# Last stage of a fused attention and expert kernel: the order of row turning, fetches, splits and SiLU work

## The chip, the cores and the metric

The kernel runs on one core of one Trainium2 chip. The metric is device microseconds of one launch, from inputs in HBM to the output in HBM. The core has a matrix engine (TensorE, "PE" in the rows), VectorE ("DVE"), ScalarE ("ACT"), GpSimd ("POOL") and the queue of SyncE ("SP") that issues most DMAs. TensorE reads weights with a separate load instruction ("PEld") that runs beside its products.

## What is computed

Three parts follow one another, all in float32, for 4 x 576 = 2304 rows of width 512:

```
p_packed = softmax_attention(p, k, v)          # 32 packed queries per head
x  = softmax_attention(q, p_packed, p_packed)  # as rows (2304, 512)
x  = sum over the 2 best of 8 experts of gate * (relu(x @ w1[e]) @ w2[e])
h  = x @ w_in                                  # 512 -> 2048
out = (h * sigmoid(h)) @ w_out                 # 2048 -> 512
```

The last two lines are the last stage, and the change touches that stage alone.

## The kernel before

To keep the precision of float32 on TensorE, every operand is held as two parts, a rounded high part and a low part ("rest" = value minus high part), and every product is three matmuls: high x high, high x rest, rest x high. ScalarE makes a high part by copying, VectorE or GpSimd the rest by subtracting. In the names of the rows a last letter h or l stands for these two.

Before the last stage, experts run one after the other (`expert_block`, line 259) and store their rows to a DRAM tensor `ys`. A row tile of the last stage (128 rows; there are 18) is fetched by two indirect DMAs of GpSimd from `ys` (`gather`, 866), gated, that is, scaled and added by ScalarE and VectorE (`gated`, 874), and turned, that is, transposed in four pieces by TensorE (`tps` in the rows) and copied out of PSUM. Fetched tiles come from a ring of five.

The last stage has two forms.

**Two blocks** of two row tiles (tiles 0 to 3; `final_block`, 837). Each has 16 steps f: a first product (12 matmuls of 256 columns, `hps<-` in the rows), the SiLU of the result (`silu_split`, 820: ScalarE's sigmoid, VectorE's product, ScalarE's high part, GpSimd's rest), the second product of the step but one before (6 matmuls of 512 columns, `acc<-`; the list `pend` with `flush`, 248, keeps it that far behind), and a hook (1302, 1308). The hook of the first block still loads and splits the output weights. Through `early(s)` (1275), with s = f in the first block and 16 + f in the second, the hooks also bring in the rows of what follows: tiles 2 and 3 for the second block, and tiles 4 to 11 for the first group. Row j is gathered at s = 1 + 2j, and gated and turned together at s = 4 + 2j. From s = 18 the turned rows of the first group are combined and split (`refill`, 918): seven operands, called 11, 21, t2, t1, t3, t4 and 22, written where the input weights of the second block were. The first pair of weights is loaded at s = 22 (`pair_load`, 964) and split at s = 26 and 28 (`pair_in`, 978).

**Two groups of super blocks** (`super_blocks`, 1046): the first group has eight row tiles (512 columns per product), the second six (384 columns). Each group has eight super blocks p = 0 to 7, one pair of hidden blocks each. A super block forms the first layer by seven products (`prod<-`) in place of eight, in Strassen's manner; sums of products are made by VectorE and GpSimd between them (u2, u3, p1, p5 and c11 in the code; `ul`, `uh` and `c` in the rows), and four SiLUs (h11, h21, h22, h12) come out. The products write two PSUM banks in turn, so a product waits until the product before last has been read. Between the products stand the output products of the super block before: chunks a0 to a3 (`acc<-`) and b0 to b3 (`y2p<-`, summed by VectorE), with j below 4 in the first group and below 3 in the second. Chunks a need h11 and h21, chunks b need h12 and h22.

During the first group the rows of the second are brought in: `rows_in` (892) gathers ahead, and one `row_in` (882) in three parts (gating; turning; copy) goes through each super block from p = 1, where p = 0 issues only the first gather; the row that is left at the end of p = 5 is done there in one go (1171). `mixed` (905) forms sums at p = 6, and `refill` splits the seven operands at p = 7: one at each of five places, and the last two at the end (1175).

**What sets the order.** From the last stage on (`M["fin"]`) every call on an engine keeps program order on that engine (`Kept`, 45). Generators are advanced with `next` at fixed places of the code, and that is the whole schedule. Engines run beside one another and wait by semaphores; an instruction that waits holds all behind it on its engine. Wrapped calls all appear under line 57, so the rows are told apart by tile names.

Of the kernel before, what the change touches and what calls it, by code (L numbers as in the profile page):

```python
# [7 lines left out]
F32 = mybir.dt.float32  # L8
# [11 lines left out]
P = 128  # L20
# [43 lines left out]
def body(ctx: ExitStack, tc: tile.TileContext, q, k, v, p, wg, wn, noise, w1, w2, w_in, w_out, out):  # L64
# [706 lines left out]
    def routed():  # L771
        ctx = mx = ExitStack()
        with mx:
# [63 lines left out]
            def final_block(m, x, hook):  # L837
                t0, n = BLOCKS[m]
                acc = [None]

                def step2(f, h):
                    if f == 0:
                        acc[0] = [pa.tile([P, DM], F32, name="acc", tag="acc") for _ in range(n)]
                    second(acc[0], h, wo, f, 15, 0)
                    if f == 15:
                        for j, y in enumerate(acc[0]):
                            store(t0 + j, A if j % 2 else V, y)
                for f in range(16):
                    ps = first(wi, x, f, n * P)
                    h = silu_split(ps, n * P)  # L850
                    flush(M["lag"])
                    pend.append(lambda f=f, h=h: step2(f, h))
                    hook(f)
# [25 lines left out]
            def staging(tags):  # L879
                box["st"] = [xp_.tile([P, 4, BW], F32, name="st", tag=tag) for tag in tags]  # L880

# [36 lines left out]
            def refill(st, xq, w, mix=None):  # L918
# [3 lines left out]
                def put(nm, src):  # L922
# [3 lines left out]
                    if type(src) is list:  # L926
                        for c in range(2):
                            A.activation(hi[:, c], src[c], AF.Copy)
                            V.tensor_tensor(lo[:, c], src[c], hi[:, c].bitcast(F32), op=OP.subtract)
                    else:  # L930
                        A.activation(hi, src, AF.Copy)
                        V.tensor_tensor(lo, src, hi.bitcast(F32), op=OP.subtract)
                    xq[nm] = [hi, lo]
                put("11", b11)
                yield
                put("21", b21)
                yield
                if mix:
                    t1, t2 = mix
                else:  # L940
                    t1 = b11
                    t2 = [mo.tile([P, DM], F32, name="t2", tag="ysb", bufs=3)[:, 0:w] for _ in range(2)]
                    V.tensor_tensor(t1, b12, b11, op=OP.subtract)
                    for c in range(2):
                        V.tensor_tensor(t2[c], b22[:, c], t1[:, c], op=OP.subtract)
                put("t2", t2)
                yield
                if mix:
                    V.tensor_tensor(b21, b21, t2, op=OP.subtract)
                else:  # L950
                    for c in range(2):
                        V.tensor_tensor(b21[:, c], b21[:, c], t2[c], op=OP.subtract)
                put("t1", t1)
                yield
                if not mix:
                    V.tensor_tensor(b12, b22, b12, op=OP.subtract)
                put("t3", b12)
                yield
                put("t4", b21)
                yield  # L960
                put("22", b22)
                yield
# [63 lines left out]
            def silu(src, h):  # L1026
# [6 lines left out]
                M["sv"] = V.tensor_tensor(src, src, sg, op=OP.mult)  # L1033
                M["sa"] = A.activation(h[0], src, AF.Copy)
# [11 lines left out]
            def super_blocks(xq, win, ro):  # L1046
# [4 lines left out]
                for g in range(last + 1):  # L1051
# [31 lines left out]
                    if g == last:  # L1083
                        next(late, None)
                        for c in ("a0", "a1", "b0", "a2", "b1", "a3", "b2", "b3"):
                            chunk(c)()
# [4 lines left out]
                    if more and p == 0:  # L1091
                        box["rows"] = rows_in(*SUPER[k + 1], ("xha", "xla"))
                    if more and p == 6:
# [16 lines left out]
                    next(late, None)  # L1110
                    next(fill, None)
                    next(wo_now)
                    if more and p < 7:
                        rows = next(box["rows"], none)
# [7 lines left out]
                    h11 = next(s11)  # L1122
                    next(s11)
# [28 lines left out]
                    next(s22)  # L1152
                    V.tensor_tensor(u3, ps, u3, op=OP.add)
                    next(fill, None)
                    s21 = silu(u3, low())
                    h21 = next(s21)
                    e = chunk("a3")
# [3 lines left out]
                    next(s21)  # L1161
# [9 lines left out]
                    if more and p == 5:  # L1171
                        for r in box["rows"]:
                            for _ in r:
                                pass
                    if p == 7 and more:
                        for _ in fill:
                            pass
                        xq = nxt
# [96 lines left out]
            def early(s):  # L1275

                j, odd = divmod(s - 1, 2)
                if not odd and 0 <= j < 2 + 2 * n0:
                    inflight[j] = gather(2 + j)
                j, odd = divmod(s - 4, 2)  # L1280
                if not odd and 0 <= j < 2 + 2 * n0:
                    y = inflight.pop(j)
                    if j < 2:
                        transposed(plain(gated(2 + j, y)), *X["c"], j)
                    else:
                        if j == 2:
                            staging(("xhb", "xlb"))
                        for _ in row_in(2 + j, y, box["st"], n0, j - 2):
                            pass
                if s == 18:  # L1290
                    win.append(refill(box["st"], xq, w0))
                if s in (18, 20, 23, 25, 27, 29, 31):
                    next(win[0], None)
                if s == 22:
                    win.append(pair_load(0))
                if s == 26:
                    win.append([])
                    win.append(pair_in(0, win[1][0], win[2]))
                if s in (26, 28):
# [14 lines left out]
            super_blocks(xq, win[2][0], win[1][1])  # L1314
# [110 lines left out]
```

## Time and profile before

| | us |
|---|---|
| median of 3 runs | 1032.12 (1029.96 to 1033.7) |
| profiled execution, its own time | 1035.61 |
| span in its profile | 1033.8 |
| TensorE busy | 962.2 (93%) |
| VectorE busy | 638.6 (62%) |
| ScalarE busy | 436.6 (42%) |
| GpSimd busy | 369.4 (36%) |
| mean granted TensorE clock | 0.97 |

Times are counted from the start of the span. The two blocks run from about 578 to 708 us, the first group from 708 to 877, the second from 877 to the end. Matmuls are pipelined, so a busy TensorE isn't one at its peak; a stall shows as an idle time in brackets, with the engine that ended it. The granted clock is a share of full speed: 1.0 is 2.4 GHz and 0.5 is 1.2 GHz.

### The profile page before, as it was taken

The numbers are of one execution on the slowest core, as the hardware profiler recorded it, in microseconds if no ns is written. First come the engines' busy times: TensorE is split into PE (matmuls) and PEld (weight loads), VectorE is DVE, ScalarE is ACT, GpSimd is POOL, SyncE is SP. The second block draws the span as 40 slices with busy tenths as digits, with TensorE's granted clock in tenths as the row PEclk, the third lists the DMA queues.
The fourth block names the chain that finished last, engine by engine and source line by source line (L and its number), as shares of the span: only waits on it lengthen the run. The fifth ranks groups of instructions, "written<-read, shape, count | busy, mean of one in ns | idle before, by whom it ended". The sixth has DMA issues, their size and how long they took to land.

```text
span 1033.8 us, 15376 instructions
## 1 busy us (share of the span) xinstructions
PE 962.2 (93%) x5716; PEld 830.4 (80%) x5716; DVE 638.6 (62%) x1157; ACT 436.6 (42%) x804; POOL 369.4 (36%) x385
## 2 busy tenths in 40 slices
PE   6999799899999999999999967798999989899997
PEld 4767678799999999999999856686788876788885
DVE  4537576567667676767444542266777777877773
ACT  3566423343434343433333443444544434544442
POOL 2163212734425161524001143424454533434442
PEclk8989899999999999999999979999999999999999
DMA  9994414575767575756233542202222211412111
GB/s 246 242 243 132 130 55 126 176 251 186 224 202 226 179 244 165 240 188 223 93 113 123 190 144 64 83 21 81 82 77 66 82 41 42 142 42 82 53 30 65
DMA packets 103554, 139.35 MB, mean 135 GB/s; under 512 B 17200, under 2 KB 66352, under 8 KB 103472
## 3 DMA queue, kind: packets, MB, share of 16 engines
q1 hardware_dynamic: 95504, 117.57, 36.5%
q0 software_dynamic: 7520, 19.93, 6.7%
q8 instruction: 47, 0.77, 0.3%
q10 hardware_dynamic: 448, 0.79, 0.2%
q14 instruction: 35, 0.29, 0.1%
HBM read 109.94 MB, written 28.31 MB: 134 GB/s over the span
## 4 chain that ended last, share of the span: by engine, by line
PE 71%; DVE 11%; ACT 6%; issue 4%; POOL 3%; DMA 3%; SPq 1%; ACTq 0%; POOLq 0%; DVEq 0%
PE acc L57 8%; PE hps L231 7%; PE hps L232 7%; PE hps L233 7%; PE acc L244 7%; PE acc L242 7%; PE acc L243 7%; PE prod L57 6%; PE hps L57 4%; PE y2p L57 4%; DVE ul L57 2%; DVE sm L57 2%; ACT sg L57 2%; POOL gl L57 2%; DVE y L57 1%
## 5 line engine op out<-in xcount | busy, mean ns | idle before, releaser
L199 POOL DMA_INDIRECT xg<-xs,idx x120 | 129.4, 1079 | 179.6 <-DVE xturn L208 145.8
L255 ACT ACTIVATE hh<-hps 128x384 fp32r<-128x384 f32 (+1 forms) x128 | 56.1, 438 | 259.3 <-PE hps L233 205.4
L256 DVE SCALAR_TENSOR_TENSOR hl<-hps,hh 128x384 fp32r<-128x384 f32 (+1 forms) x128 | 62.4, 487 | 107.2 <-ACT hh L255 92.1
L57 POOL TENSOR_TENSOR gl<-sg,gh 128x256 fp32r<-128x256 f32 x32 | 26.9, 843 | 87.4 <-ACT gh L57 58.1
L57 DVE TENSOR_TENSOR ul<-ul,sg 128x512 f32<-128x512 f32 (+1 forms) x32 | 26.8, 837 | 24.3 <-ACT sg L57 24.3
L57 PE MATMUL y2p<-wb5h,g 128*128 128x512 f32 x112 | 39.3, 393 | 0.2 <-POOL g L57 0.2
L57 PE MATMUL y2p<-wb4h,g 128*128 128x512 f32 x112 | 39.3, 391 | 0.0
L57 DVE TENSOR_TENSOR sg<-hps,sg 128x256 f32<-128x256 f32 x32 | 13.5, 422 | 41.5 <-ACT sg L57 41.5
L57 POOL TENSOR_TENSOR gl<-ul,gh 128x512 fp32r<-128x512 f32 (+1 forms) x16 | 30.5, 1904 | 20.4 <-ACT gh L57 20.4
L57 POOL DMA_INDIRECT y<-ys,slots x32 | 31.9, 998 | 12.3 <-DMA raw<-wf_out 5.2
L57 DVE TENSOR_TENSOR y<-y,y2p 128x512 f32<-128x512 f32 x42 | 28.6, 681 | 12.5 <-PE y2p L57 12.5
L57 POOL TENSOR_TENSOR g<-uh,g 128x512 fp32r<-128x512 f32 (+1 forms) x16 | 20.7, 1293 | 38.7 <-ACT g L57 38.7
L57 PE MATMUL tps<-ident,y 128*128 128x128 f32 x64 | 10.9, 297 | 24.4 <-DVE y L57 24.4
L57 ACT ACTIVATE sg<-ul 128x512 f32<-128x512 f32 (+1 forms) x32 | 18.5, 579 | 34.1 <-POOL ul L57 33.9
L219 POOL DMA_INDIRECT xg<-xs,idx x10 | 9.9, 992 | 60.9 <-DVE hl L256 28.9
L57 PEld LDWEIGHTS tps<-ident,y 128*128 128x128 f32 x64 | 7.6, 150 | 29.8 <-issue 26.2
L813 POOL DMA_INDIRECT y<-ys,slots x4 | 4.6, 1157 | 73.4 <-DVE hl L256 72.5
L57 POOL TENSOR_TENSOR ul<-ul 128x512 f32<-128x512 f32 (+1 forms) x16 | 19.1, 1192 | 32.0 <-DVE ul L57 32.0
L57 POOL TENSOR_TENSOR g<-ul,g 128x512 fp32r<-128x512 f32 (+1 forms) x16 | 19.0, 1189 | 31.4 <-ACT g L57 20.6
L57 PE MATMUL acc<-wb5h,gl 128*128 128x512 f32 x64 | 25.9, 405 | 4.5 <-POOL gl L57 4.5
L57 POOL TENSOR_TENSOR gl<-c,gh 128x512 fp32r<-128x512 f32 (+1 forms) x16 | 18.5, 1157 | 28.3 <-ACT gh L57 23.0
L57 PE MATMUL acc<-wb4h,gl 128*128 128x512 f32 x64 | 25.6, 400 | 2.7 <-POOL gl L57 2.7
(686 smaller groups left out, 3479.8 us busy)
## 6 DMA issues: line engine op xcount, KB each, us to landing
raw<-in_moe_w_dram SPq DMA_DIRECT2D x56, 512.0 KB
raw<-wf_out SPq DMA_DIRECT2D x24, 512.0 KB
ys<-ysb SPq DMA_DIRECT2D x40, 256.0 KB
raw<-in_moe_w_in_dram SPq DMA_DIRECT2D x16, 512.0 KB
raw<-in_moe_w_out_dram SPq DMA_DIRECT2D x16, 512.0 KB
raw<-wf_in SPq DMA_DIRECT2D x32, 256.0 KB
xs<-xr SPq DMA_DIRECT2D x18, 256.0 KB
km<-in_k_dram SPq DMA_DIRECT2D x8, 512.0 KB
```

The costliest lines, as they stand in the source:

```text
L57: ins = fn(*args, **kw)
L199: G.indirect_dma_start(out=xg[:, g * P:(g + 1) * P], out_offset=None, in_=xs[:, :].rearrange("n (a f) -> (n a) f", a=4), in_offset=bass.In ...
L219: G.indirect_dma_start(out=xg[:, :], out_offset=None, in_=src, in_offset=bass.IndirectOffsetOnAxis(ap=ix[:, c:c + 1], axis=0))
L231: T.matmul(ps, wh[:, c, s], xh[:, c, :n], start=c == 0, stop=False)
L232: T.matmul(ps, wh[:, c, s], xl[:, c, :n], start=False, stop=False)
L233: T.matmul(ps, wl[:, c, s], xh[:, c, :n], start=False, stop=c == 3)
L242: T.matmul(y, hh[:, s], wh[:, f % 2, :], start=f == 0, stop=False)
L243: T.matmul(y, hh[:, s], wl[:, f % 2, :], start=False, stop=False)
L244: T.matmul(y, hl[:, s], wh[:, f % 2, :], start=False, stop=f == last)
L255: A.activation(hh, ps, AF.Relu)
L256: V.scalar_tensor_tensor(hl, ps, 0.0, hh.bitcast(F32), op0=OP.max, op1=OP.subtract)
L813: G.indirect_dma_start(out=y[c][:, :], out_offset=None, in_=src, in_offset=bass.IndirectOffsetOnAxis(ap=slots[:, t, c:c + 1], axis=0))
```

## The change

In the two blocks, row j is gathered at s = 2 + 2j, gated at s = 5 + 2j and turned at s = 6 + 2j, so gating and turning stand in different steps. At the very first step both pending second products of the last expert are flushed. The parts of the first group's `refill` are spread over single steps; its last two splits (t4 and 22) move into the first super block, which takes the generator as `fill0`. The first pair of weights is loaded at s = 19 and split at s = 22 and 24. The first fetch of the second group is issued at s = 24, and its rows go through p = 0 to 5.

In the second group's `refill`, a rest is made one place after its high part, and the rests of 21, t3 and 22 are GpSimd's; the last two splits are made in the next group's first super block. In every super block the sum u3 stands ahead of the SiLU product of h22, and the high part and rest of h21 ahead of those of h22. After the last super block, the b chunk of the last tile comes third instead of last.

```
 final_block
-                    flush(M["lag"])
+                    flush(0 if f == m == 0 else M["lag"])
...
 refill: put
-                        V.tensor_tensor(lo, src, hi.bitcast(F32), op=OP.subtract)
+                        e = G if mix and nm in ("21", "t3", "22") else V
+                        rest.append(lambda: e.tensor_tensor(lo, src, hi.bitcast(F32), op=OP.subtract))
+                        if not mix:
+                            rest.pop()()
...
+                rest = []
+                def again():
+                    if rest:
+                        rest.pop(0)()
                 put("11", b11)
                 yield
+                again()
                 put("21", b21)
                 yield
                 if mix:
+                    again()
                     t1, t2 = mix
+                    put("t2", t2)
+                    yield
+                    again()
+                    put("t1", t1)
+                    yield
+                    again()
+                    V.tensor_tensor(b21, b21, t2, op=OP.subtract)
+                    put("t3", b12)
...
                 yield
+                again()
                 put("t4", b21)
                 yield
+                again()
                 put("22", b22)
+                yield
+                again()
                 yield
...
 silu
-                M["sv"] = V.tensor_tensor(src, src, sg, op=OP.mult)
-                M["sa"] = A.activation(h[0], src, AF.Copy)
+                V.tensor_tensor(src, src, sg, op=OP.mult)
+                yield
+                A.activation(h[0], src, AF.Copy)
                 G.tensor_tensor(h[1], src, h[0].bitcast(F32), op=OP.subtract)
                 yield
...
 super_blocks
-                        for c in ("a0", "a1", "b0", "a2", "b1", "a3", "b2", "b3"):
+                        for c in ("a0", "a1", f"b{prev['n'] - 1}", "a2", "a3", "b0", "b1", "b2")[:5 + prev["n"] - 1]:
...
-                    if more and p == 0:
+                    if p == 0:
+                        fill = fill0
+                    if g and more and p == 0:
                         box["rows"] = rows_in(*SUPER[k + 1], ("xha", "xla"))
+                        next(box["rows"])
...
-                    if more and p < 7:
-                        rows = next(box["rows"], none)
+                    if more and p < 6:
+                        rows = next(box["rows"])
                         next(rows, None)
...
                     ps = product(wt["t4"], x["t4"])
                     e()
-                    next(s22)
                     V.tensor_tensor(u3, ps, u3, op=OP.add)
-                    next(fill, None)
                     s21 = silu(u3, low())
                     h21 = next(s21)
+                    next(s22)
+                    next(s21)
+                    next(s21)
+                    next(s22)
+                    next(fill, None)
                     e = chunk("a3")
                     e2 = chunk("b2")
                     ps = product(wt["22"], x["22"])
                     e()
-                    next(s21)
                     e2()
...
-                    if more and p == 5:
-                        for r in box["rows"]:
-                            for _ in r:
-                                pass
                     if p == 7 and more:
-                        for _ in fill:
-                            pass
-                        xq = nxt
+                        fill0, xq = fill, nxt
...
 early
-                j, odd = divmod(s - 1, 2)
-                if not odd and 0 <= j < 2 + 2 * n0:
-                    inflight[j] = gather(2 + j)
-                j, odd = divmod(s - 4, 2)
+                j, odd = divmod(s - 6, 2)
                 if not odd and 0 <= j < 2 + 2 * n0:
                     y = inflight.pop(j)
                     if j < 2:
-                        transposed(plain(gated(2 + j, y)), *X["c"], j)
+                        transposed(plain(y), *X["c"], j)
                     else:
                         if j == 2:
                             staging(("xhb", "xlb"))
-                        for _ in row_in(2 + j, y, box["st"], n0, j - 2):
-                            pass
+                        turn_in(y, box["st"], n0, j - 2)
+                j, odd = divmod(s - 5, 2)
+                if not odd and 0 <= j < 2 + 2 * n0:
+                    inflight[j] = gated(2 + j, inflight[j])
+                j, odd = divmod(s - 2, 2)
+                if not odd and 0 <= j < 2 + 2 * n0:
+                    inflight[j] = gather(2 + j)
                 if s == 18:
                     win.append(refill(box["st"], xq, w0))
-                if s in (18, 20, 23, 25, 27, 29, 31):
+                if s == 24:
+                    box["rows"] = rows_in(*SUPER[1], ("xha", "xla"))
+                    next(box["rows"])
+                if s in (18, 20, 25, 26, 27, 28, 29, 30, 31):
                     next(win[0], None)
+                if s == 19:
+                    win.append(pair_load(0))
                 if s == 22:
-                    win.append(pair_load(0))
-                if s == 26:
                     win.append([])
                     win.append(pair_in(0, win[1][0], win[2]))
-                if s in (26, 28):
+                if s in (22, 24):
                     next(win[3])
```

`turn_in` is the new name of the turning and copying half of `row_in`. Where `refill` has no `mix` (the first group), its sums and splits are the same, with a `yield` between each.

## Rows read from the trace of the kernel before

**Rows 1.** Windows: stretch, length, busy PE, PEld, DVE, ACT, POOL, clock, DMA share, GB/s.
```profile
592.90:707.60 114.70, 91.95 (x543) 80.61 (x544) 47.66 (x68) 47.14 (x92) 43.95 (x50) 0.93 0.26 79
707.60:730.90 23.30, 19.29 (x72) 14.30 (x71) 16.57 (x21) 11.43 (x19) 9.90 (x8) 0.85 0.29 90
853.00:876.80 23.80, 21.64 (x91) 16.41 (x90) 17.67 (x25) 10.17 (x17) 7.25 (x5) 1.00 0.14 44
876.80:901.30 24.50, 20.75 (x91) 17.55 (x92) 21.81 (x30) 14.09 (x24) 11.14 (x8) 0.93 0.35 118
```

**Rows 2.** Waits of TensorE (total, times, longest): 578 to 707.6, 731 to 901.3, 901.3 to 1030.
```profile
PE tps L57 <- DVE y L57: 20.9, 10, 3.6
...
PE tps L57 <- DVE y L57: 2.6, 1, 2.6
...
PE acc L57 <- POOL gl L57: 5.8, 7, 0.9
```

**Rows 3.** Timeline, one row turned in the first block (start us, us, engine; idle before).
```profile
635.93 1.02 DVE L57 SCALAR_TENSOR_TENSOR y<-y,gates,y 128x512 f32<-128x512 f32 x1 [1.10 <-ACT y L57]
637.10 0.63 PE L57 MATMUL tps<-ident,y 128*128 128x128 f32 x4 [1.82 <-DVE y L57]
637.49 0.36 PE L57 MATMUL hps<-xha,wa6h 128*128 128x256 f32 x1
```

**Rows 4.** Chain that ended last, a step without a row turned (start us, us, what).
```profile
682.45 1.43 PE hps L57 x12
683.88 1.39 PE acc L57 x6
```

**Rows 5.** Timeline, the first row's fetch and its gating.
```profile
590.64 0.96 POOL L57 DMA_INDIRECT y<-ys,slots  x1 [5.21 <-DMA raw<-wf_out]
591.90 0.95 POOL L57 DMA_INDIRECT y<-ys,slots  x1 [0.30 <-issue]
596.84 0.70 ACT L57 ACTIVATE y<-y,gates 128x512 f32<-128x512 f32 x1
```

**Rows 6.** Timeline around the first super block and the first row of the next.
```profile
704.92 1.04 ACT L57 ACTIVATE wa6h<-st 128x1024 fp32r<-128x1024 f32 x1
709.21 0.59 ACT L57 ACTIVATE uh<-prod 128x512 f32<-128x512 f32 x1
709.34 1.23 DVE L57 TENSOR_TENSOR wb4l<-raw,wb4h 128x1024 fp32r<-128x1024 f32 x1 [1.50 <-ACT wb4h L57]
728.86 1.30 DVE L57 SCALAR_TENSOR_TENSOR y<-y,gates,y 128x512 f32<-128x512 f32 x1 [0.39 <-ACT y L57]
730.31 0.63 PE L57 MATMUL tps<-ident,y 128*128 128x128 f32 x4 [0.91 <-DVE y L57]
```

**Rows 7.** Chain that ended last, one first-layer product of each group.
```profile
745.95 1.36 PE prod L57 x6
...
906.27 1.04 PE prod L57 x6
```

**Rows 8.** Timeline, h21 in one super block of the second group.
```profile
914.28 0.33 PE L57 MATMUL prod<-wa5h,wb2l 128*128 128x384 f32 x1
914.33 0.53 ACT L57 ACTIVATE sg<-ul 128x384 f32<-128x384 f32 x1 [1.50 <-POOL ul L57]
915.36 0.55 DVE L57 TENSOR_TENSOR ul<-prod,ul 128x384 f32<-128x384 f32 x1
918.20 1.90 POOL L57 TENSOR_TENSOR gl<-ul,gh 128x384 fp32r<-128x384 f32 x1 [1.11 <-ACT gh L57]
920.15 0.50 PE L57 MATMUL acc<-wb5h,gl 128*128 128x512 f32 x1 [0.90 <-POOL gl L57]
```

**Rows 9.** Groups by form (xcount, busy, mean ns, idle before): GpSimd 730 to 1030, VectorE 900 to 1020.
```profile
L57 POOL TENSOR_TENSOR gl<-c,gh 128x384 fp32r<-128x384 f32 x8 | 8.2, 1020 | 11.6 <-ACT gh L57 11.6
...
L57 DVE TENSOR_TENSOR c<-c,sg 128x384 f32<-128x384 f32 x7 | 3.9, 559 | 4.1 <-ACT sg L57 4.1
```

**Rows 10.** Timeline, ScalarE's queue at the end: two half stores of the last row tile.
```profile
1028.23 1.18 ACTq L862 DMA_DIRECT2D out_dram<-osb  x2
```

## What the change should do to the time

> **What bounds the kernel now.** I read the stretches of the last stage first: share of TensorE and granted clock in each. Four of them hold idle or half-clock time [rows 1]. Then TensorE's waits, by stage: three causes recur [rows 2]. Then the timeline around one instance of each, to see what the late engine did just before.
>
> In the two first blocks (592.9 to 707.6 us) TensorE waits 20.9 us, ten times, for VectorE's y, once per row turned [rows 2]. One instance shows the order: ScalarE's scaling of y, VectorE's 1.02 us sum, the transposes 1.82 us late, and the next step's first product only 0.39 us after the transposes begin [rows 3]. All stand at the end of one step and in program order, so TensorE can't overtake. With no row to turn a step lasts 2.82 us, 1.43 us for the first product and 1.39 for the second of an earlier one [rows 4]. So that stretch needs 27 steps x 2.82 = 76.1, two last second products at 1.39 [rows 4] = 2.8, the rest of a step begun earlier 0.9 (four of its six matmuls) and ten transpose groups x 0.39 = 3.9: **83.7 us**. It takes 114.7, so 31.0 us are lost: 20.9 in these waits, the rest mostly in steps at the lower clock level (mean granted clock 0.93 there, of which 1.0 is 2.4 GHz and 0.5 is 1.2 GHz) [rows 1].
>
> **The change, part by part.**
>
> *Rows a step behind their gates.* Gather moves from step 1 + 2j to 2 + 2j, gating from 4 + 2j to 5 + 2j, turning to 6 + 2j. Nothing is added: ten rows, the same gathers, gatings, transposes. The y that ends 1.02 + 0.15 us before the transposes today would end a full 2.82 us step earlier, so the 1.82 us wait has 1.0 us in hand. What is late next? The gather still has three steps to its gate, about 8.5 us once no step is stretched; the row of the first gather ends issuing at 592.85 and ScalarE uses its data at 596.84 without a recorded wait, 4.0 us later [rows 5]: enough. GpSimd's order is rest of the SiLU, then two gathers (0.95 us each and 0.3 between [rows 5]); the first product of a step reaches its own second product two steps later, so the rest may come some 3 us late. The tiles of a fetch are a ring of five, so the second gather of row j + 2 waits for the transposes of row j in the same step; they come before GpSimd gets there. The first fetch comes one step later, and the last expert's stores, whose products move ahead of one first product, 1.43 us earlier; so what is left of today's 5.21 us in GpSimd's queue [rows 5], with the SiLU rest queued behind it, is about 1 us. Weight loads for the second product keep their step, but steps are shorter, so a load that is issued two steps ahead has about 5.7 us; ScalarE may wait there at a few steps. SP is passed by one pair of weight loads (step 22 to 19) whose tiles are free by then. Ends: -31 (every loss gone) to -20 (loads and gathers bind in a third of the steps); I take **-28**, near the whole, as the dense steps at 682 us carried all the splits of the second block. Those splits (earlier weight pair in steps 22 and 24, sums and splits one to a step from 25) cost nothing: VectorE is busy 47.66 of 114.7 us here [rows 1] and no step gets more than its 2.82 us but step 22, whose excess of a few tenths is caught up in the next. The same holds for the first fetch of the second group at step 24, 2.2 us of GpSimd.
>
> *Two splits and the first row moved into the first super block.* This adds to a stage where VectorE is the bottleneck (16.57 of 23.3 us busy, clock 0.85 [rows 1]). Each split is a ScalarE copy of 1.04 us and a VectorE rest of 1.23 (a weight rest of the same width), the gating 1.30 us on VectorE [rows 6]. Counted from the first product's start at 707.6 [rows 1]: its copy out ends at +2.2 as now (709.80 [rows 6]); the split's copy then +3.3, its rest +4.5, the weight rest (1.23) +5.8, the gated row +7.0. TensorE has finished two products (1.36 each [rows 7]) at +2.8 and now meets the transposes: a new wait of **4.2 us**, with five products queued behind it. The second split holds the sum that frees a bank for the fifth product 1.23 us more, a second wait of about 2.5. Part of this replaces today's own waits there. Following the queue on, the next super block reaches its transposes at about +26.5, against 730.31 - 707.6 = +22.7 now [rows 6]. Ends: 0 (the work slips under existing idle time, and the low clock is as long as today) to +8 (the 4.2 us again at the lower clock). I take **+4**.
>
> *The row left for the end of step 5* no longer waits: **-2.6** [rows 2].
>
> *Change of group.* Its two super blocks take 23.8 and 24.5 us [rows 1]; dense they need 15 x 1.36 = 20.4 and 7 x 1.04 + 8 x 1.39 = 18.4 [rows 4, 7], so 9.5 us are lost. Seven rests on VectorE become four, three go to GpSimd, and two of the seven operands are split in the next super block instead of all at the border, each rest one step after its ScalarE copy. VectorE gives up about 3 us and the waits for ScalarE. On GpSimd a two-input 128x384 operation takes 1.02 us and on VectorE 0.56 [rows 9]; a rest is 128x768, so about 2.0 us there, 6 us in all, beside 7.25 and 11.14 busy of 24 [rows 1]: room enough. Ends: -9 to 0; I take **-6**: a third stays, for rests that GpSimd ends later than VectorE would. The Trainium skill, "GPSIMD Reference", 4.1 Engine selection, says to keep two-input elementwise work on VectorE, GpSimd being about twice as slow; the rows agree (1.8 times), and by it alone this part would be a loss (+2, the case below). I follow the rows on which engine has time.
>
> *Sums ahead of SiLU products.* In the second group each super block but the last waits 0.9 us for the rest of h21 [rows 2, 8]. Today the sum stands behind VectorE's product for h22 and runs 915.36 to 915.91, and GpSimd's rest for h21 918.20 to 920.10. After: the fourth product has ended by 914.61, while the sigmoid of h22 runs (914.33, 0.53 us) [rows 8]; the sum ends 915.3, the second sigmoid 915.8, both VectorE products (0.56 each [rows 9]) 916.5, the copy 917.0, so the rest starts at 917.1. That is 1.1 us earlier for a need at 920.15 - 0.90 = 919.25 [rows 8], even if it keeps its 1.90 us. The h22 rest, now second, is needed a product of 1.04 and one of 1.39 us later still. Waits sum to 5.8 [rows 2]; ends -6 to -3, taken **-5**.
>
> *Tail.* The row with two half stores goes earlier; the two issues at the end (1.18 us [rows 10]) become one: **-0.4**, between 0 and -1.
>
> Sum: -28 + 4 - 2.6 - 6 - 5 - 0.4 = **-38.0**. The profiled execution took 1035.6 us (span 1033.8 and 1.8 around it), 3.5 over the median 1032.1. It gives 997.6; against the median, **994.1 us**.
>
> **Rivals.**
>
> *The blocks meet a new limit.* Loads or gathers come too late for the short steps and half of the 28 stays. For: a transfer share of 0.26 that comes in bursts [rows 1]; against: the 4.0 us landing. -14 + 4 - 2.6 - 6 - 5 - 0.4 = -24: 1008. Chance 0.14.
>
> *The moved splits cost more.* The first super block loses 12, as VectorE's backlog runs on into the next with the low clock: -30: 1002. For: the clock of 0.85 in that stretch today. Chance 0.13. GpSimd's rests binding at the border (three of 2.0 us each replacing shorter ones of VectorE on TensorE's path, +2 instead of -6) also gives 1002; chance 0.06. This is what the Trainium skill's rule above ("GPSIMD Reference", 4.1 Engine selection) would mean.
>
> *Slower.* The ring of five: if row j's transposes come after GpSimd reaches the second gather, GpSimd holds the SiLU rests, the second products wait, and so the transposes. It decides once a rest comes more than about 3 us late. Each row would then cost two steps, 5.6 us: 56 instead of 31 lost, +25, and with the other parts (-10) +15: 1047. Against: transposes precede the gather by almost a microsecond. Chance 0.03.
>
> *The change does nothing in the blocks.* If gates are late because gathers are, the wait only moves from TensorE's y to ScalarE's: -10 in all: 1022. Chance 0.03.
>
> **Numbers.** The likeliest case has 0.61 and its own range 987 to 1001. Down to 985 all ends but the extreme fit; up to 1010 takes in the next three rivals. About 0.3% is what a measurement of this kernel can tell from no change, 3 us; only the slower case lies above, and a sum of the mild misses might fall near zero. Faster 0.95, same 0.02, slower 0.03.
>
> **What would show it.** Right: no waits of TensorE for y before the super blocks; that stretch near 85 us at clock 1.0; a new wait of some 4 us for y in the first super block; none at the end of its sixth; two border super blocks near 21 us each; second-group super blocks of 15.9 instead of 16.8 us. Wrong: TensorE waiting for the SiLU rest or ScalarE for a load in the blocks, a first super block over 30 us, GpSimd's rests named as releasers at the border.

## The result, and the profile after

The changed kernel took **994.96 us** (median of 4 runs, 993.96 to 996.18), beside 1031.04 us (4 runs) for the kernel before: a ratio of 0.9653, 95% interval 0.962 to 0.9686, so 36.1 us less. The profiled execution took 996.18 us with a span of 994.4.

Busy time of each engine, from the page of the kernel after:

```profile
PE 948.1 (95%) x5716; PEld 821.6 (83%) x5716; DVE 639.4 (64%) x1154; ACT 434.3 (44%) x804; POOL 379.6 (38%) x388
```

TensorE is busy 14 us less than before with the same products, at a mean granted clock of 0.99 instead of 0.97; the rest of the gain is idle time. VectorE's total is the same within a microsecond, and GpSimd has some 10 us more. So no work was saved; the order changed what waits.

Windows of the kernel after, in the columns of [rows 1]. They are, in order: the two blocks from their first product on; the first super block; the eighth and last of the first group; the first three of the second group.

```profile
574.84:677.97 103.13, 100.65 (x636) 90.40 (x634) 49.17 (x76) 53.13 (x104) 52.71 (x56) 0.98 0.38 121
677.97:696.30 18.33, 12.53 (x47) 9.03 (x46) 11.48 (x17) 9.44 (x15) 4.53 (x4) 0.91 0.28 84
824.42:844.82 20.40, 20.40 (x91) 16.89 (x90) 17.79 (x24) 11.62 (x19) 11.41 (x8) 1.00 0.16 53
844.82:864.84 20.02, 19.13 (x91) 16.17 (x90) 18.56 (x23) 10.59 (x19) 10.93 (x8) 1.00 0.32 101
864.84:882.52 17.68, 15.93 (x79) 14.00 (x78) 14.01 (x23) 8.47 (x16) 6.43 (x6) 1.00 0.37 124
882.52:898.37 15.85, 15.85 (x80) 14.01 (x79) 12.70 (x21) 7.70 (x15) 7.32 (x6) 1.00 0.21 66
```

The same blocks of the kernel before:

```profile
578.18:707.57 129.39, 106.63 (x636) 93.58 (x635) 55.57 (x78) 55.60 (x106) 47.33 (x54) 0.93 0.29 92
```

The blocks went from 129.39 to 103.13 us, and TensorE is busy in all but 2.5 of them. The eighth super block, busy for all of its 20.40 us, is dense. Two places are not: the first super block (12.53 busy of 18.33, clock 0.91) and the second of the second group, 17.68 us, where the next one needs 15.85.

TensorE's waits in the kernel after (total, times, longest): for the blocks, then the first two super blocks, then from the change of group to the end. Between 721 and 844 us there is none.

```profile
PE tps L57 <- DVE y L57: 2.2, 1, 2.2
PE acc L57 <- POOL gl L57: 0.3, 1, 0.3
...
PE tps L57 <- DVE y L57: 5.0, 2, 3.5
PE prod L57 <- DVE ul L57: 1.5, 2, 1.0
PE acc L57 <- POOL gl L57: 0.8, 1, 0.8
PE prod L57 <- DVE uh L57: 0.8, 1, 0.8
...
PE prod L57 <- DVE uh L57: 1.7, 1, 1.7
...
```

Of the ten waits for y of [rows 2] one is left (two in run 10, a second profile of this kernel), the 2.6 us are gone, and so are the seven for h21's rest. New are the wait of 3.5 us for y in the first super block and one of 1.7 us after the change of group. The first super block's other waits, 2.3 us together, stand where the kernel before had 3.1. One turned row of the first block in the timeline after, to be read against [rows 3] (start, length, engine; idle before):

```profile
622.68 0.75 DVE L57 SCALAR_TENSOR_TENSOR y<-y,gates,y 128x512 f32<-128x512 f32 x1 [1.10 <-ACT y L57]
624.70 0.60 PE L57 MATMUL tps<-ident,y 128*128 128x128 f32 x4
```

VectorE still waits 1.10 us for ScalarE, but y ends at 623.43, 1.27 us ahead of the transposes.

The time by stretches, from the start of one super block to the next in both traces:

| stretch | predicted | measured | before to after |
|---|---|---|---|
| two blocks | -28 | -26.3 | 129.39 to 103.13 |
| first super block | +4 | +3.9 | 14.40 to 18.33 |
| super blocks 3 to 7 (the row of step 5) | -2.6 | -2.9 | 107.2 to 104.3 |
| eighth super block and the next two | -6 | -5.8 | 63.87 to 58.1 (first -7.8, then +2.0) |
| second group from there to TensorE's end | -5 | -5.8 | 5 x 0.98, then 0.9 |
| after TensorE's end | -0.4 | +0.8 | |
| sum | -38.0 | -36.1 | |

The second super block takes about 23.8 us in both. The profiled spans differ by 39.4 us, since the blocks begin 3.3 us earlier in the profile of after (574.84 against 578.18), behind code that the change doesn't touch. In the profiles of the runs below that start lies anywhere between 572.88 and 585.51. Why isn't known; stretches are therefore compared from the blocks' first product on.

### The profile page after: what moved, and what is told of

The parts are those of the page before. It is cut to its first block, busy times and chain, and to the rows that moved or that the text cites. A ratio compares the mean times of both kernels' runs of the same rounds, so it can differ in the third digit from the quotient of the medians.

```text
span 994.4 us, 15365 instructions
## 1 busy us (share of the span) xinstructions
PE 948.1 (95%) x5716; PEld 821.6 (83%) x5716; DVE 639.4 (64%) x1154; ACT 434.3 (44%) x804; POOL 379.6 (38%) x388
## 5 line engine op out<-in xcount | busy, mean ns | idle before, releaser
L57 POOL TENSOR_TENSOR gl<-ul,gh 128x512 fp32r<-128x512 f32 (+1 forms) x16 | 24.9, 1557 | 49.4 <-ACT gh L57 49.4
L57 POOL DMA_INDIRECT y<-ys,slots x32 | 35.2, 1100 | 7.4 <-issue 5.5
L813 POOL DMA_INDIRECT y<-ys,slots x4 | 4.7, 1178 | 73.3 <-DVE hl L256 72.4
L57 POOL TENSOR_TENSOR ul<-ul 128x512 f32<-128x512 f32 (+1 forms) x16 | 19.1, 1192 | 28.8 <-DVE ul L57 28.8
L57 POOL TENSOR_TENSOR uh<-uh,ul 128x512 f32<-128x512 f32 (+1 forms) x16 | 18.8, 1174 | 22.8 <-ACT ul L57 21.0
L57 PEld LDWEIGHTS y2p<-wb5h,g 128*128 128x128 f32 x112 | 20.9, 188 | 6.7 <-POOL g L57 1.3
L57 PE MATMUL acc<-wb5l,gh 128*128 128x512 f32 x64 | 25.1, 393 | 0.0
L57 PE MATMUL acc<-wb4l,gh 128*128 128x512 f32 x64 | 25.1, 392 | 0.0
```

What stands on the lines that cost most here:

```text
L57: ins = fn(*args, **kw)
L813: G.indirect_dma_start(out=y[c][:, :], out_offset=None, in_=src, in_offset=bass.IndirectOffsetOnAxis(ap=slots[:, t, c:c + 1], axis=0))
```

## Experiments

Each edit is made to the changed kernel. Several effects are smaller than what a median can tell, so the stretches of the traces are read too. The kernel before took 1033.09 us beside the first four, 1038.52 beside the fifth to eighth and 1030.98 beside the last three: across these groups, compare ratios, with 0.9653 for the changed kernel.

**1. Gating and turning in one step again.**

```
-                    y = inflight.pop(j)
+                    y = gated(2 + j, inflight.pop(j))
...
-                j, odd = divmod(s - 5, 2)
-                if not odd and 0 <= j < 2 + 2 * n0:
-                    inflight[j] = gated(2 + j, inflight[j])
```

> The changed kernel, but each row is gated in the step in which it is turned, just ahead of the transposes; fetches and all else as changed. Theory (the step between gate and turn removed the waits): ten waits of TensorE for y come back, 1.8 to 2.2 us each, and some time at the lower clock: the first super block starts 18 to 27 us later, 1013 to 1022 us. Rival (the gain of the blocks came from the later first fetch and the spread splits): within 5 us of 995.

1014.75 us, ratio 0.9821 (0.9794 to 0.9848). The blocks' window and TensorE's waits in it:

```profile
574.77:697.03 122.26, 102.60 (x635) 90.14 (x634) 49.32 (x76) 53.24 (x104) 52.33 (x56) 0.97 0.32 102
```

```profile
PE tps L57 <- DVE y L57: 19.3, 10, 5.1
```

All ten waits are back, and the blocks take 122.26 us where the changed kernel needs 103.13. With fetch, weight loads and splits as in the changed kernel, the step between gate and turn is worth 19.1 us; the other 7 of the 26.3 belong to the rest of the change, which this run doesn't divide. Run 2 shows that the first fetch isn't among it; the spread sums and splits and the earlier weight pair were not tried alone.

**2. First fetch and both second products as before.**

```
-                    flush(0 if f == m == 0 else M["lag"])
+                    flush(M["lag"])
...
-                if not odd and 0 <= j < 2 + 2 * n0:
-                    inflight[j] = gather(2 + j)
+                if s == 1 or not odd and 1 <= j < 2 + 2 * n0:
+                    inflight[max(j, 0)] = gather(2 + max(j, 0))
```

> The changed kernel, but row 0 is fetched at step 1 and the last expert's second product is not flushed ahead. Theory: the fetch stands in GpSimd's queue for the stores, the rest of one SiLU comes late, one wait of about 2 us: 996 to 999 us. Rival (the first fetch was worth more, as the late rest also drops the clock): over 1000 us. Second rival: no difference, within 1 us of 995.

995.18 us, ratio 0.9629 (0.96 to 0.9658); blocks 102.5 us. TensorE's waits in the blocks:

```profile
PE acc L57 <- POOL gl L57: 1.7, 1, 1.7
PE tps L57 <- DVE y L57: 1.5, 2, 1.0
```

The SiLU rest behind GpSimd's fetch is late again, by 1.7 us instead of 0.3, and the waits for y are shorter, 1.5 us instead of 2.2 (3.2 in run 10's profile of the changed kernel): one small wait was exchanged for another. The blocks took 103.13 and 102.78 us in the two profiles of the changed kernel. So the second rival holds: these two lines of the change do nothing to the time that can be told.

**3. All rests on VectorE.** The rests stay one place behind their high parts.

```
-                        e = G if mix and nm in ("21", "t3", "22") else V
+                        e = V
```

> The changed kernel, but all seven rests of the second group's rows are VectorE's again, still one place after their copies. Theory (VectorE is what the change of group waits for): the two super blocks at the border grow by 2 to 5 us together, 997 to 1000 us. Rival, which is what the Trainium skill's page GPSIMD Reference, section 4.1 Engine selection, would mean (VectorE does such work in half the time): they shrink by 1 to 3 us, 992 to 994 us.

994.16 us, ratio 0.9622 (0.96 to 0.9644). The medians can't tell it from the changed kernel; the trace can: the first super block of the second group takes 19.48 us instead of 20.02 and the second 15.65 instead of 17.68. The timeline of the changed kernel shows both places:

```profile
852.38 1.85 POOL L57 TENSOR_TENSOR wa4l<-st,wa4h 128x768 fp32r<-128x768 f32 x1
852.48 2.18 DVE L57 TENSOR_TENSOR c<-c,sg 128x384 f32<-128x384 f32 x1 [0.72 <-ACT sg L57]
...
855.29 1.11 POOL L57 TENSOR_TENSOR gl<-c,gh 128x384 fp32r<-128x384 f32 x1 [1.05 <-ACT gh L57]
855.44 0.55 DVE L57 TENSOR_TENSOR uh<-prod,uh 128x384 f32<-128x384 f32 x1
...
857.87 2.03 POOL L57 TENSOR_TENSOR wa6l<-st,wa6h 128x768 fp32r<-128x768 f32 x1
858.12 2.07 DVE L57 TENSOR_TENSOR sm<-raw 128x256 f32<-128x256 f32 x1
...
866.19 0.69 DVE L57 TENSOR_TENSOR osb<-y2p,y 128x512 f32<-128x512 f32 x1 [1.29 <-DMA out_dram<-osb]
...
868.59 0.55 DVE L57 TENSOR_TENSOR uh<-prod,uh 128x384 f32<-128x384 f32 x1
869.19 0.44 PE L57 MATMUL prod<-wa1h,wb2h 128*128 128x384 f32 x1 [1.75 <-DVE uh L57]
```

The same operations with the rests on VectorE:

```profile
853.65 0.56 DVE L57 TENSOR_TENSOR c<-c,sg 128x384 f32<-128x384 f32 x1 [0.59 <-ACT sg L57]
...
857.67 0.41 DVE L57 TENSOR_TENSOR sm<-raw 128x256 f32<-128x256 f32 x1
859.28 0.95 DVE L57 TENSOR_TENSOR wa6l<-st,wa6h 128x768 fp32r<-128x768 f32 x1
...
863.74 0.69 DVE L57 TENSOR_TENSOR osb<-y2p,y 128x512 f32<-128x512 f32 x1
```

Two VectorE operations that start just after a rest on GpSimd (by 0.10 and 0.25 us) take 2.18 us instead of 0.56 and 2.07 instead of 0.41; they end 0.43 and 0.29 us after that rest, as if they made little headway until then. The one that reads a product out of PSUM keeps its 0.55 us beside GpSimd. So a rest moved away costs VectorE some 1.6 us of stretching, where the rest itself takes it 0.95. The backlog then meets a tile that a store still holds (1.29 us), and TensorE waits 1.75 us. The Trainium skill, "GPSIMD Engine Reference", 1 Specifications, says that GpSimd shares its SBUF interfaces with VectorE, with contention from VectorE instructions that have two SBUF inputs; the two stretched rows are such operations and the third isn't, so the trace agrees.

Which of the two engines is stretched goes by which starts first. Here are the same two operations, a weight rest on VectorE and a SiLU rest on GpSimd, in the second super block of the second group, first in run 1 and then in run 10:

```profile
885.63 1.22 DVE L57 TENSOR_TENSOR wb3l<-sm,wb3h 128x1024 fp32r<-128x1024 f32 x1
885.68 2.02 POOL L57 TENSOR_TENSOR g<-ul,g 128x384 fp32r<-128x384 f32 x1
...
869.85 1.01 POOL L57 TENSOR_TENSOR g<-ul,g 128x384 fp32r<-128x384 f32 x1
869.91 2.03 DVE L57 TENSOR_TENSOR wb3l<-sm,wb3h 128x1024 fp32r<-128x1024 f32 x1
```

VectorE ahead by 0.05 us keeps its 1.22 us and GpSimd takes 2.02; GpSimd ahead by 0.06 us keeps its 1.01 and VectorE takes 2.03. TensorE waits there for the next sum on VectorE, so this super block takes 16.72 us in run 1 and 17.66 in run 10, though both kernels have the same code there. Runs 2 and 5 lie with the first (16.67 and 16.76), the profile of after and run 7 with the second (17.68 and 17.64). So of the 2.0 us from 17.68 to 15.65 about one hangs on this order; the moved rests, with the tile wait behind them, cost the other. It fits that the rest of h21 takes 1.90 us in [rows 8] where such an operation takes 1.02 in [rows 9]: a weight rest on VectorE had started 0.17 us ahead of it.

**4. SiLU products in the old order, in every super block.**

```
+                    next(s22)
+                    next(s22)
                     V.tensor_tensor(u3, ps, u3, op=OP.add)
                     s21 = silu(u3, low())
                     h21 = next(s21)
-                    next(s22)
-                    next(s21)
-                    next(s21)
-                    next(s22)
...
                     e()
+                    next(s21)
+                    next(s21)
                     e2()
```

> The changed kernel, but with the old order in each super block: SiLU product, high part and rest of h22 ahead of the sum u3, and those of h21 after the seventh product. Theory: the wait of 0.9 us for the rest of h21 returns in each super block of the second group, about six of them: 5 to 7 us more, 1000 to 1002 us, and nothing in the first group. Rival (those waits went because VectorE came into the second group less late): no difference, within 1 us of 995.

1005.04 us, ratio 0.9719 (0.9688 to 0.9749). TensorE's waits from 880 to 1000 us:

```profile
PE acc L57 <- POOL gl L57: 5.7, 7, 0.9
```

The seven waits are back almost to the tenth, and the second group's super blocks take 16.82 us again. Beyond that the first super block is 1.4 us longer, where nothing was expected, and the first of the second group 1.3, where VectorE's queue is full as well. So the order is worth 10.1 us in the medians and 7.1 in the traces, counted from the blocks' first product to the end, against the -5 that the prediction gave it for the second group alone.

**5. First row of the second group gated in the blocks.** It is then turned in the first super block.

```
+                if s == 30:
+                    box["r0"] = next(box["rows"])
+                    next(box["r0"])
...
                     if more and p < 6:
-                        rows = next(box["rows"])
-                        next(rows, None)
+                        if g:
+                            rows = next(box["rows"])
+                            next(rows, None)
+                        else:
+                            rows = box["r0"]
```

> The changed kernel, but the first row of the second group is gated at step 30 of the blocks and only turned in the first super block. Theory (in the first super block VectorE's queue is the bound, and the gating is only one piece of it): TensorE's wait of 3.5 us for y goes, but most comes back at the next products; the first super block shrinks by 0.8 to 1.8 us. Rival (that wait is a loss of its own): it shrinks by 3 us or more.

1003.08 us, ratio 0.9655 (0.9592 to 0.9717): no gain over the changed kernel. The first super block takes 17.63 instead of 18.33 us, a little less gain than expected. The wait for y is gone, but 2.4 us of waiting for `ul` and 1.5 for `c` come in its place: `c` stands behind two rests in VectorE's queue, `ul` behind a split's copy in ScalarE's, so the splits delay whatever is next. And a 1.3 us wait for a SiLU rest appears in the last steps of the blocks, where GpSimd now issues the next fetch; the blocks take 104.35 us.

**6. Stores take tiles from the ring of five**, idle by then, instead of the ring of three.

```
-                osb = mo.tile([P, DM], F32, name="osb", tag="xg" if end else "ysb", bufs=5 if end else 3)
+                osb = mo.tile([P, DM], F32, name="osb", tag="xg" if t > 3 else "ysb", bufs=5 if t > 3 else 3)
```

> The changed kernel, but the output tiles of the groups use the ring of five that the fetched rows leave free, instead of a ring of three. Theory (at the change of group VectorE waits for a store to free a tile, and a sum that TensorE needs stands behind it): the wait of TensorE for that sum in the ninth-from-first super block of the groups (1.75 us in the changed kernel's profile, 0.8 in two other runs) goes: 1 to 2 us less in that super block. Rival (VectorE is late there anyway, from GpSimd's rests): no difference, under 0.4 us.

1002.78 us, ratio 0.966 (0.9601 to 0.9718). The super block of 17.68 us takes 16.25; the one before stays at 20.01. VectorE's wait for the store is gone from the trace. Without this edit the super block takes 16.67 to 17.68 us, by which engine starts first (run 3), so the tile held by a store is worth 0.4 to 1.4 us of that loss; the rest is the late VectorE, which run 3 removes.

**7. The two splits back at the end of the blocks.**

```
+                if s == 31:
+                    next(win[0], None)
+                    next(win[0], None)
```

> The changed kernel, but the splits t4 and 22 are made at the last step of the blocks, as before the change. Theory (the two splits, not the gating alone, lengthen the first super block, and the blocks have VectorE time to spare): the first super block shrinks from 18.3 to 15 to 16.5 us, its start stays within 0.5 us, 992 to 993.5 us in all. Rival (the splits then run on into the first super block and nothing is won): it stays at 18 us.

996.57 us, ratio 0.9601 (0.9545 to 0.9657). Windows of the blocks and the first super block:

```profile
578.09:680.86 102.77, 99.31 (x636) 89.00 (x634) 49.47 (x76) 54.61 (x106) 52.77 (x56) 1.00 0.38 121
680.86:695.47 14.61, 10.67 (x48) 7.97 (x46) 12.20 (x17) 7.76 (x14) 5.88 (x4) 1.00 0.33 106
```

The first super block is 3.7 us shorter and its clock is at the full level, and the blocks are not longer. Moving these splits out of the blocks was a loss; the blocks had cover for them.

**8. Runs 3, 5, 6 and 7 together.**

> The changed kernel with the rests on VectorE, the first row gated early, the ring of five for stores and the splits t4 and 22 in the blocks. If the effects add: about 2.6 less at the border (rests and stores), 4 less in the first super block: 987 to 990 us. If VectorE's queue bounds the first super block whatever is moved: 991 to 993 us.

993.73 us, ratio 0.9576 (0.9524 to 0.9627). First super block 13.29 us, the first two of the second group 19.46 and 15.65: the effects add. From the blocks' first product to the end of the span it is 412.25 us, against 419.56 and 418.92 in the two profiles of the changed kernel. The 1.3 us wait at the end of the blocks (run 5) stays.

**9 and 10. A version without the losses, and the changed kernel beside it.** Run 9 has the edits of runs 3, 6 and 7, gates the second group's first row at s = 28, and gates every row ahead of the weight split of its step: `gate` is the gating taken out of `early`. The edits of those runs are left out below, and so is `gate` in the second block's hook.

```
+                    gate(f)
                     tick()
...
+                if s == 28:
+                    box["r0"] = next(box["rows"])
+                    next(box["r0"])
...
+                    if more and p < 6:
+                        if g:
+                            rows = next(box["rows"])
+                            next(rows, None)
+                        else:
+                            rows = box["r0"]
                     next(wo_now)
-                    if more and p < 6:
-                        rows = next(box["rows"])
-                        next(rows, None)
```

> The changed kernel with what the runs so far favour: all rests on VectorE, splits t4 and 22 at the last step of the blocks, ring of five for stores; the first row of the second group gated at step 28 (at step 30 its fetch held GpSimd: 1.3 us at the end of the blocks); and in every step or super block the gating ahead of the weight split (in the blocks) or of the weight rest (in the groups). Theory (each remaining wait for y comes from the weight work ahead of the gating on VectorE): against the changed kernel, 3.7 to 5 us less in the first super block, 1.5 in the second, 2.6 at the border, 2 to 3 in the blocks: 9 to 12 us less, 983 to 986 us. Rival (the waits move on to the next product): 5 to 7 us less.

> The changed kernel itself once more, on the same chip as the run beside it: 993 to 997 us.

Run 9 took **985.8 us** (984.56 to 988.06, 5 runs), ratio 0.9558 (0.9528 to 0.9588); the changed kernel on the same chip 995.1, ratio 0.9636 (0.9605 to 0.9666). So it beats both kernels, the changed one by 9.3 us. Windows of run 9 (blocks, first super block, first and second of the second group):

```profile
572.88:675.24 102.36, 100.40 (x636) 90.40 (x635) 51.95 (x77) 55.00 (x107) 54.39 (x56) 0.98 0.40 127
675.24:688.93 13.69, 10.75 (x48) 7.97 (x46) 11.43 (x16) 7.03 (x13) 4.01 (x3) 1.00 0.22 74
836.83:856.29 19.46, 19.04 (x91) 16.14 (x90) 18.15 (x27) 10.57 (x20) 6.13 (x6) 1.00 0.38 121
856.29:871.93 15.64, 15.64 (x79) 14.06 (x78) 12.93 (x21) 7.81 (x15) 7.27 (x6) 1.00 0.39 119
```

And of the changed kernel beside it:

```profile
578.38:681.16 102.78, 99.31 (x635) 89.01 (x634) 49.47 (x76) 53.02 (x104) 52.73 (x56) 1.00 0.39 121
681.16:699.64 18.48, 13.27 (x48) 9.88 (x46) 11.59 (x17) 9.34 (x15) 4.81 (x4) 0.82 0.29 83
848.14:868.14 20.00, 19.13 (x91) 16.15 (x90) 18.56 (x23) 10.59 (x19) 10.89 (x8) 1.00 0.33 100
868.14:885.80 17.66, 15.94 (x79) 13.99 (x78) 14.15 (x23) 8.47 (x16) 6.43 (x6) 1.00 0.36 126
```

The gain lies in the first super block (-4.8) and at the change of group (-0.5 and -2.0). The blocks give 0.4 where 2 to 3 were expected, and the second super block 0.2 where 1.5 was. Gating ahead of the split thus did little: it ends the wait of 1.0 us for the second row's y (run 10), but run 9 still waits 2.0 us for the first row's.

**11. The sum first, but h22's rest ahead of h21's.**

```
-                    next(s21)
-                    next(s21)
                     next(s22)
...
                     e()
+                    next(s21)
+                    next(s21)
```

> The changed kernel, but only the sum u3 stands ahead of the SiLU product of h22; high part and rest of h22 stay ahead of those of h21. Theory (GpSimd's rest of h22 ahead of that of h21 is the larger half): 0.2 to 0.9 us more in each super block of the second group, between this kernel's 15.85 and 16.8. Rival (the sum alone is what counts): 15.85 in each.

995.2 us (2 runs), ratio 0.9647 (0.9605 to 0.9689). TensorE's waits from 880 to 1000 us:

```profile
PE acc L57 <- POOL gl L57: 1.3, 7, 0.2
```

The waits fall from 5.7 to 1.3 by the sum alone, and a super block from 16.82 to 16.10 us; the order of the two rests gives the other 0.26. The sum's place is the larger part, and all of what the whole time shows: 995.2 us beside 995.1 for the changed kernel, as the change of group is 0.4 shorter this way and so is the last super block.

## Why the prediction was right, and where it was not

**Rows a step behind their gates: right, in mechanism and size.** The prediction put 1.0 us in hand for y; the row above shows 1.27. What it did not see is that the term could not reach its end of -31. The first row, and in run 10 the second too, comes late: in the timeline after, the weight split of that step stands ahead of the first gating in both queues.

```profile
595.71 1.04 ACT L57 ACTIVATE wb5h<-raw 128x1024 fp32r<-128x1024 f32 x1
596.66 0.70 ACT L57 ACTIVATE y<-y,gates 128x512 f32<-128x512 f32 x1
596.79 1.23 DVE L57 TENSOR_TENSOR wb5l<-raw,wb5h 128x1024 fp32r<-128x1024 f32 x1 [1.44 <-ACT wb5h L57]
...
598.82 0.63 PE L57 MATMUL tps<-ident,y 128*128 128x128 f32 x4 [2.16 <-DVE y L57]
```

The prediction looked behind the gates (fetch, loads, ring) but not at what is queued ahead of them. This split isn't the whole cause for the first row, though: run 9 gates ahead of it, and its wait is still 1.96 us.

```profile
592.43 1.25 DVE L57 TENSOR_TENSOR wb4l<-raw,wb4h 128x1024 fp32r<-128x1024 f32 x1 [1.43 <-ACT wb4h L57]
...
596.09 0.63 PE L57 MATMUL tps<-ident,y 128*128 128x128 f32 x4 [1.96 <-DVE y L57]
```

There the scaling of y (594.36) stands behind a SiLU's high part on ScalarE, whose product on VectorE (593.60) stood behind the rest of an earlier weight split. No run shows how much of the 1.96 us comes from that. "A new limit" falls with the 26.3 us and the 0.3 us of waiting for a SiLU rest, "nothing in the blocks" and the slower ring with run 1.

**First super block: right in size and place.** It forecast a 4.2 us wait for y with two products done. The timeline after:

```profile
681.18 1.23 DVE L57 TENSOR_TENSOR wa5l<-st,wa5h 128x1024 fp32r<-128x1024 f32 x1 [2.95 <-ACT wa5h L57]
...
683.46 0.75 DVE L57 SCALAR_TENSOR_TENSOR y<-y,gates,y 128x512 f32<-128x512 f32 x1
684.35 0.63 PE L57 MATMUL tps<-ident,y 128*128 128x128 f32 x4 [3.50 <-DVE y L57]
```

The wait is 3.50 us; y ends 6.2 us after the super block's first product, where +7.0 was worked out, since the gating took 0.75 and not the 1.30 of [rows 6]. With no GpSimd operation beside it the gating is shorter; in [rows 6] a SiLU rest on GpSimd had started 0.57 us ahead of it. The second wait of "about 2.5" was 0.76, 0.95 and 0.59. The rival of a 12 us loss falls.

**Change of group: the size right, the reason half wrong.** -5.8 against -6, but it is -7.8 in two super blocks and +2.0 in the next. In runs 1, 2 and 5, where VectorE starts first, that next one is only +1.0 to +1.1 (run 3), so that the size agrees this closely is luck. The step that failed is "VectorE gives up about 3 us": GpSimd had the time that [rows 1] showed, and yet its rests cost VectorE more than they took off it (run 3: some 1.6 us each against 0.95). "GpSimd's rests binding at the border" is the rival that had the sign of this edit: without them the stretch is 1.5 to 2.6 us shorter still. The rule that the prediction set aside (the Trainium skill, "GPSIMD Engine Reference", 4.1 Engine selection) was right for this edit, though not by the price that it names, the longer time on GpSimd, but by what VectorE paid. The whole part gained even so: the gain belongs to the spread splits, the later rests and the new place of the sums, which run 3 keeps. The sums give some 1.4 us of it (run 4); the other two were not tried apart. As an indicator, "GpSimd's rests named as releasers" failed: the damage shows as longer VectorE rows, not as a wait for GpSimd. The +2.0 was in no term.

**Sums ahead: right.** -4.9 in five super blocks, and another -0.9 in the last, which the prediction had left out, for -5. Run 4 shows that the order also shortens both crowded stretches, which the prediction did not count. There its gain is part of the other terms.

**Tail: not seen.** From the end of the last sum to the end of the span it is 5.6 us before and 5.5 to 6.4 in four profiles with the changed tail (after, 9, 10 and 11), so -0.4 can't be told from nothing; the +0.8 of the table lies within that spread.

The whole came out 1.9 us short of the predicted gain, nearly all of it the blocks (1.7). That the total agrees so closely is also luck of signs: tail +1.2 against second group -0.8.

## What to carry to other kernels

Where one engine's result is used in the same step in which it is made, move the producer one step ahead, and check both what stands behind it and what is queued ahead of it, in that step and in the ones before. Before moving work into a later stage, ask whether the earlier one still has cover: the two splits cost 3.7 us in the first super block and nothing in the blocks. Idle time of another engine is not free capacity when operations of the two stretch each other; look whether neighbouring rows grow, and which of the two starts first.

## What the runs showed of the hardware

- Where a VectorE operation with both inputs in SBUF and a GpSimd subtraction overlapped, the one that started second was stretched past the end of the first. With GpSimd first, its 128x768 rests took 1.85 and 2.03 us, near the 2.0 worked out from [rows 9], and the VectorE operations 2.18 and 2.07 instead of 0.56 and 0.41. With VectorE first by 0.05 us (run 1), VectorE's took 1.22 us and GpSimd's 2.02 instead of 1.01. A start that moves by a tenth of a microsecond can so change which engine pays, and moved a super block between 16.7 and 17.7 us.
- In the first super block the same stall of TensorE came out at two mean granted clocks, 0.91 after and 0.82 in run 10, with all but the same length (18.33 and 18.48 us). The stall was 3.50 us in both; after it the clock was 0.55 from 684.72 to 688.40 us in the one and 0.50 from 687.40 to 692.50 in the other, and in the one the second wait of 0.76 us came on top. In run 7, without the splits, the longest wait in this super block was 1.8 us and the clock stayed at 1.00.
- The start of the blocks moved between 572.88 and 585.51 us from profile to profile, with the same code ahead of it, and between 572.88 and 578.38 in the last three runs, which share a chip. The wider spread is a third of the whole gain, and its cause stays open.
